# Roots of the first pairs one pair at a time, later v loads behind a later root, their maxima spread through a line of memory, and later batches' value products five units behind the scores

## The chip, the cores and the metric

The kernel is one program on one core of a Trainium2 chip. The metric is the device time of one execution in microseconds, lower is better. The core has a matrix engine (PE, whose weight loads are listed apart as PEld), three engines for elementwise work and reductions (DVE, ACT, POOL), and SP, which here only issues transfers. Every engine, and every queue of transfers, takes its instructions in the order in which the program lists them; an instruction that has to wait holds up all that stand behind it on its engine.

## The reference, cut to what matters

```python
# attention: batch 4, heads 12, seq S = 448, head dim D = 64
q_n, k_n = rmsnorm(q, g_q), rmsnorm(k, g_k)
scores = (1 / sqrt(D)) * q_n @ k_n.transpose(0, 1, 3, 2)
attn = softmax(scores, axis=-1)
x = (attn @ v), laid out as [1792 tokens, 768]
# first feed-forward, w_in [768, 2048], w_out [2048, 768]
h = x @ w_in;  g = h * sigmoid(1.702 * h);  y = g @ w_out
# second feed-forward, its own w_in and w_out of the same shapes
h = y @ w_in2;  g = maximum(h, 0) + alpha * minimum(h, 0);  out = g @ w_out2
```

`rmsnorm(x, g)` is `x / sqrt(mean(x*x) + 1e-6) * g` over the 64 elements of a head.

## The kernel before

**Stages.** Attention works on pairs of heads: NP = 6 pairs in each of the B = 4 batches, four units to a pair. Batch 0 runs first, in f32, while the weights of the first feed-forward arrive as 8-byte words and are rebuilt: `from_words` (ACT L147, DVE L163 and L164), the largest value of each piece (DVE L244) and a split into two 16-bit halves (ACT L178, DVE L179). Then the first feed-forward of batch 0 runs, with the attention of batch 1 filled in between its products, then that of batch 1 with the attention of batch 2, and so on; the second feed-forward comes last. The order of every engine is made by a list scheduler from the program as it is written; the order of a queue is that of its issuing engine.

**The first pairs.** For each pair ACT squares q and k, DVE sums the squares (L403, tile `ss`), POOL turns the sums into reciprocal roots with a first guess and three rounds of four small operations (`normalize`, L404 to L414, tile `rs`), DVE multiplies (L438, tile `qn`), PE transposes (L445, L447, tile `qt`) and ACT brings the result to its place (L448). Then PE makes the scores (L496). `normalize` can take several pairs at once: pairs 0 and 1 have a chain of POOL operations each, pairs 2 and 3 share one, and so do pairs 4 and 5. `rooted[P]` is the last operation of the chain of pair P.

**The later v's.** All of v of batches 1 to 3 is read once in advance for its largest magnitude: `v_scale` loads 8 pieces of 168 KB per batch on POOL's queue (L310) into the two buffers of `vst`, and ACT takes the magnitudes' sum in `t` with a column of results (L311). `v_scales` then reduces the columns on DVE (L299), rounds to a power of two (L104, L105), and `partition_max` spreads the largest over all partitions: a diagonal on DVE (L117, `diag`), a product with ones on PE (L119, `pm`), a maximum on DVE (L120), then a reciprocal (L111, L112). This stands in the program once for batch 0, once for each of batches 1 to 3 and in a few places for weights. The loads may begin after `rooted[1]`. The scale of batch 0's v is needed for `first_sc` (DVE L656), which ACT uses to write `x` (L139), the input of the first product of the feed-forward (PE L727, `hp`).

**Later batches.** For a unit PE makes scores (L505, tile `sp`), DVE the row maximum (L510, `nm`), ACT the exponent (L529, `pr`) and the upper half (L571, `ph`), DVE the lower half (L598), SP issues the transpose of `ph` into `pt` (two buffers), and PE multiplies with v (L626, `xp`). Within `attention` a step is one unit; the values of a pair of units are written LAG_ = 4 steps behind their scores:

```python
last = min(NU, 4 * NP * (b + 2)) + LAG
while done < min(want, NU + LAG):
    next(att_steps)
```

Each batch's feed-forward has 56 ticks over which its attention steps are spread. `yp` (L796) is the second product of the first feed-forward, `hp` of L727 and L773 the first.

Of the kernel before, what the change touches and what calls it, by code (L numbers as in the profile page):

```python
# [9 lines left out]
F32 = mybir.dt.float32  # L10
# [4 lines left out]
ALU = mybir.AluOpType  # L15
# [3 lines left out]
VN = 8  # L19
# [4 lines left out]
W1O_AFTER = 4  # L24
VLAG = 0
LAG_ = 4
PACE = (1.0, 1.0, 1.0, 1.0)
HOLD = 12800
M_AT = 2
# [27 lines left out]
def attention_moe_kernel(  # L57
# [215 lines left out]
    g_col = const.tile([128, 1], F32, name="g_col")  # L273
    mv = const.tile([128, B], F32, name="mv")
    av = const.tile([128, B], F32, name="av")

    def gains():
        gq = small.tile([128, D], F32, tag="gq", name="gq", bufs=1)
# [25 lines left out]
    def v_scale(b):  # L304
        flat = v[b].rearrange("h s d -> (h s d)").rearrange("(p n) -> p n", p=128)
        n = flat.shape[1] // VN
        col = small.tile([128, VN], F32, tag="vcol", name="vcol")
        for i in range(VN):
            t = raw_p.tile([128, n], F32, tag="vst", name="vst")
            nc.gpsimd.dma_start(out=t, in_=flat[:, i * n:(i + 1) * n])  # L310
            nc.scalar.activation(out=t, in_=t, func=AF.Abs, accum_out=col[:, i:i + 1])  # L311
        v_scales(b, col)

    raws = {}
    rawv = {}
# [348 lines left out]

    def attention(us):

        for i in range(len(us) + LAG):
            if 0 < i <= len(us):
                high(us[i - 1])
            if i < len(us):  # L670
                scores(us[i])
                exponent(us[i])
            if 2 <= i <= len(us) + 1:
                low(us[i - 2])
            if i >= LAG and us[i - LAG] % 2 == 1:
                values(us[i - LAG] // 4, us[i - LAG] % 4 // 2)
            yield

    def first_pairs():

        steps = attention([4 * P + r for P in range(NP) for r in range(2)])
        for i, _ in enumerate(steps):
            P, r = divmod(i, 2)
            if P >= NP:
                yield
                continue
            if r == 0:
                prep = prep_pair(P + 1) if P + 1 < NP else iter(())
            next(prep, None)
            if r == 0 and P % 2 == 0 and P + 2 < NP:  # L690
                normalize(P + 2, P + 3)
            if r == 1:
                if P + 1 + QKB < NP:
                    load_qk(P + 1 + QKB)
                if P + 3 < NP:
                    load_v(P + 3)
            yield
# [456 lines left out]
    if True:  # L1154
        make_identity(nc, ident)
        nc.vector.memset(ones, 1.0)
        nc.vector.tensor_copy(out=identf, in_=ident)
        load_qk(0)
        gains()
        load_v(0)  # L1160
        load_qk(1)
        load_v(1)
        g0 = big.tile([128, KF, 2, S], F16, tag="g", name="g0")
        stage = g0.rearrange("p m e t -> p (m e t)").bitcast(F32)
        parts = stage[:, 0:R1I * 1024].bitcast(I32).rearrange("p (i n t) -> p i n t", i=R1I, t=2)
        raw1o = g0.rearrange("p m e t -> p m (e t)").bitcast(I32)[:, KF - 4 * R1O:, FIRST:].rearrange("p m (n t) -> p m n t", t=2)

        def num1i(j):
            if j == KD - 1:
                return stage[:, 5120:5120 + FF]  # L1170
            return held.bitcast(F32)[:, (j - 3) * FF:(j - 2) * FF]

        def num1o(j):
            if j == KF - 2:
                return att_p.tile([128, 2 * NT2 * D], F32, tag="ph", name="num1o", bufs=PHB)[:, 0:DM]
            return raw_p.tile([128, 2 * NT2 * D], F32, tag="qk", name="num1o", bufs=QKB)[:, 0:DM]

        w1i_steps = weights(
            moe_w_in, "w1i", lambda: w1i, later_rows(w1i, 3, num1i), lambda t: parts[:, t % R1I], 4, R1I, 2.0 ** -14, scales,
            G1I  # L1180
        )
        w1o_steps = weights(
            moe_w_out, "w1o", lambda: w1o, later_rows(w1o, 2, num1o), lambda t: raw1o[:, 4 * (t % R1O):4 * (t % R1O) + 4], 2,
            R1O, 2.0 ** -25, scales, G1O
        )
        next(w1i_steps)
        normalize(0)
        for _ in prep_pair(0):
            pass
        for P in range(2, 1 + QKB):  # L1190
            load_qk(P)
        load_v(2)
        normalize(1)
        for _ in first_pairs():
            for _ in range(W_RATE):
                next(w1i_steps, None)
        for _ in w1i_steps:
            pass
        v_scales(0, v0)
        first_x()  # L1200
        moe1_scales(0)
        for P in range(NP, NP + 2):
            load_qk(P)
            load_v(P)
        n1o = 0
        steps = attention([4 * P + r for P in range(NP) for r in range(2, 4)])
        for i, _ in enumerate(steps):
            pairs = max(0, (i - LAG + 1) // 2)
            rows = KF - 2 if pairs >= 4 else (HOLD + pairs * HELD) // (2 * DM) - 2
            while n1o < min(1 + 2 * rows + 3 * (rows // 2), (i + 1) * W1O_RATE, 57):  # L1210
                next(w1o_steps)
                n1o += 1
            if i >= M_AT and i - M_AT < KF:
                first_in(slice(0, FIRST), i - M_AT, g0, None)
            if i == VS_AT:
                for b in range(1, B):
                    with tc.issue_after(rooted[1].ins):
                        v_scale(b)
        while n1o < 57:
            next(w1o_steps)  # L1220
            n1o += 1
        for m in range(len(range(2 * NP + LAG)) - M_AT, KF):
            first_in(slice(0, FIRST), m, g0, None)
        with tc.issue_after(loads["w1o"][W1O_HOLD].ins):
            normalize(NP, NP + 1)
            for _ in prep_pair(NP):
                pass
            load_qk(NP + 2)
            load_qk(NP + 3)
            load_v(NP + 2)  # L1230
        att_steps = other_batches()
        done = 4 * NP
        late = late_weights(ctx, att)
        for b in range(B):
            last = min(NU, 4 * NP * (b + 2)) + LAG
            first = done
            got = None
            for i, _ in enumerate(moe1(b) if b else first_moe1(g0)):
                lead = 0 if b else B1_AT
                want = first + (last - first) * min(1.0, max(0.0, i + 1 - lead) / (PACE[b] * TICKS - lead))  # L1240
                while done < min(want, NU + LAG):
                    next(att_steps)
                    done += 1
                if b == B - 1:
                    for _ in range(1 if i < 2 * KF else 2):
                        if got is None or i >= 2 * KF:
                            got = next(late, None)
        second_layer(late)
# [30 lines left out]
```

## Time and profile before

| | |
|---|---|
| Time, median of 3 runs | 1167.9 us (1166.9 to 1169.97) |
| Profiled execution, its own time | 1169.73 us |
| its span in the trace | 1168.0 us |
| mean granted clock of PE | 0.961 |
| PE, busy share of the span | 92% |
| DVE | 69% |
| ACT | 58% |
| POOL | 15% |

The span is what the trace covers, and the time has 1.73 us more around it. The busy shares are means over stages that differ; times below are counted from the start of the span. A granted clock of 1.00 is 2.4 GHz, and the other level is 1.2 GHz.

### The profile page before, as it was taken

The numbers are of one execution on the slowest core, as the hardware profiler recorded it, in microseconds if no ns is written. First come the engines' busy times: TensorE is split into PE (matmuls) and PEld (weight loads), VectorE is DVE, ScalarE is ACT, GpSimd is POOL, SyncE is SP. The second block draws the span as 40 slices with busy tenths as digits, with TensorE's granted clock in tenths as the row PEclk, the third lists the DMA queues.
The fourth block names the chain that finished last, engine by engine and source line by source line (L and its number), as shares of the span: only waits on it lengthen the run. The fifth ranks groups of instructions, "written<-read, shape, count | busy, mean of one in ns | idle before, by whom it ended". The sixth has DMA issues, their size and how long they took to land.

```text
span 1168.0 us, 18355 instructions
## 1 busy us (share of the span) xinstructions
PE 1072.6 (92%) x6755; PEld 586.6 (50%) x6755; DVE 810.1 (69%) x1407; ACT 682.0 (58%) x1396; POOL 169.6 (15%) x336
## 2 busy tenths in 40 slices
PE   3587779778998999999999999999999999999998
PEld 1243447743444445545555455444444477666665
DVE  6979987897788976567633957499977222978351
ACT  4789666576888886578733554256545323645220
POOL 3321001575543432210000000000000000000000
PEclk9677889998999999999999999999999999999999
DMA  7975542358898876665555801555533413353011
GB/s 244 273 213 143 148 136 71 89 100 165 173 175 171 148 121 143 139 120 97 102 123 155 302 4 52 201 202 195 183 103 120 138 68 120 100 179 105 29 32 31
DMA packets 235274, 158.05 MB, mean 135 GB/s; under 512 B 167728, under 2 KB 214448, under 8 KB 235184
## 3 DMA queue, kind: packets, MB, share of 16 engines
q1 hardware_dynamic: 228912, 141.21, 46.5%
q0 software_dynamic: 6272, 15.67, 5.2%
q8 instruction: 53, 0.87, 0.3%
q14 instruction: 37, 0.30, 0.1%
HBM read 92.22 MB, written 25.69 MB: 101 GB/s over the span
## 4 chain that ended last, share of the span: by engine, by line
PE 49%; DVE 17%; DMA 13%; ACT 10%; issue 7%; POOL 3%; SPq 1%; ACTq 0%; DVEq 0%; POOLq 0%
PE op L1062 16%; PE h L902 10%; PE yp L796 10%; PE hp L773 5%; ACT pr L529 3%; PE xp L626 2%; DVE ph L598 2%; DVE nm L510 2%; DMA w2raw<-in_moe_w_in_dram 2%; DMA g<-in_moe_w_out_dram 2%; ACT ph L571 2%; DVE g L140 1%; DMA t<-hl 1%; PE hp L727 1%; DMA yr<-y_dram 1%
## 5 line engine op out<-in xcount | busy, mean ns | idle before, releaser
L796 PE MATMUL yp<-g,w1o 128*128 128x448 f16 x1152 | 228.3, 356 | 0.6 <-DVE g L737 0.6
L902 PE MATMUL h<-x,w2i 128*128 128x512 f16 (+1 forms) x1152 | 220.6, 354 | 3.5 <-DVE rm_w2o L104 2.2
L773 PE MATMUL hp<-x,w1i 128*128 128x448 f16 x864 | 169.8, 353 | 1.8 <-DVE t L782 1.8
L902 PEld LDWEIGHTS <-w2i 128*128 128x128 f16 x1152 | 113.1, 98 | 110.0 <-issue 6.3
L796 PEld LDWEIGHTS <-w1o 128*128 128x128 f16 x1152 | 110.2, 98 | 112.5 <-issue 14.1
L773 PEld LDWEIGHTS <-w1i 128*128 128x128 f16 x864 | 81.9, 98 | 83.9 <-issue 9.9
L598 DVE SCALAR_TENSOR_TENSOR ph<-pr,sm,ph 128x448 f16<-128x448 f32 x126 | 89.6, 739 | 27.6 <-ACT ph L571 27.4
L510 DVE TENSOR_REDUCE nm<-sp 128x2 f32<-128x896 f32 x96 | 92.5, 964 | 10.5 <-PE sp L505 8.4
L907 ACT ACTIVATE pos<-h,sign 128x512 f32<-128x512 f32 (+1 forms) x64 | 40.1, 628 | 91.8 <-PE h L902 84.7
L529 ACT ACTIVATE pr<-sp,nm,c_s 128x448 f32<-128x448 f32 x126 | 90.1, 718 | 3.8 <-DVE ph L598 2.2
L571 ACT ACTIVATE ph<-pr,sm 128x448 f16<-128x448 f32 x126 | 77.9, 660 | 18.1 <-DVE sm L568 18.0
L1062 PEld LDWEIGHTS <-even 128*128 128x128 f16 x672 | 65.7, 98 | 43.4
L908 DVE SCALAR_TENSOR_TENSOR pos<-h,slope,pos 128x512 f32<-128x512 f32 (+1 forms) x64 | 43.4, 680 | 61.0 <-ACT pos L907 61.0
L727 PE MATMUL hp<-x,w1i 128*128 128x256 f16 (+1 forms) x576 | 63.2, 270 | 10.1 <-DVE g L737 7.6
L1062 PEld LDWEIGHTS <-odd 128*128 128x128 f16 x504 | 49.3, 98 | 32.6
L626 PE MATMUL xp<-pt,vs 128*64 128x256 f16 (+1 forms) x792 | 48.6, 268 | 17.4 <-DMA pt<-ph 15.1
L1062 PE MATMUL op<-w2lo,even 128*128 128x384 f16 x384 | 63.4, 326 | 0.0
L727 PEld LDWEIGHTS <-w1i 128*128 128x128 f16 x576 | 53.8, 102 | 18.5 <-issue 13.8
L505 PE MATMUL sp<-t 64*128 64x448 f16 (+1 forms) x432 | 54.6, 360 | 0.9 <-ACT pr L529 0.9
L626 PEld LDWEIGHTS <-vs 128*64 128x64 f16 x792 | 38.6, 113 | 33.0 <-DMA pt<-ph 14.6
L512 ACT ACTIVATE nm<-nm,c_s 128x2 f32<-128x2 f32 x72 | 20.9, 290 | 47.5 <-DVE nm L510 47.3
L1062 PE MATMUL op<-w2hi,even 128*128 128x384 f16 x288 | 47.5, 326 | 0.0
(239 smaller groups left out, 1650.0 us busy)
## 6 DMA issues: line engine op xcount, KB each, us to landing
g<-in_moe_w_in_dram SPq DMA_DIRECT2D x24, 512.0 KB, 5.4
g<-in_moe_w_out_dram SPq DMA_DIRECT2D x32, 384.0 KB, 3.7
w2raw<-in_moe_w_in_dram SPq DMA_DIRECT2D x24, 512.0 KB, 5.6
w2raw<-in_moe_w_out_dram SPq DMA_DIRECT2D x16, 768.0 KB, 6.3
g_dram<-pos SPq DMA_DIRECT2D x48, 256.0 KB, 2.0
gp<-g_dram SPq DMA_DIRECT2D x8, 1024.0 KB, 7.1
odd<-g_dram SPq DMA_DIRECT2D x6, 1024.0 KB, 5.4
y_dram<-y SPq DMA_DIRECT2D x24, 224.0 KB, 2.6
```

Of the source, the lines that this page charges most:

```text
L505: nc.tensor.matmul(out=sp[:, j, 0:S] if n == 2 else sp[ds, 0, 0:S], lhsT=qt[ds] if n == 2 else qt[ds, 64:128], rhs=kt[ds, 0:S], start=(i = ...
L510: nc.vector.tensor_reduce(out=nm[:, 0:n], in_=sp[:, 0:n, 0:S], op=ALU.max, axis=AX, negate=True)
L529: nc.scalar.activation(out=pr[i], in_=sp[:, i, 0:S], func=AF.Exp, bias=nm[:, i:i + 1], scale=c_s if u >= 4 * NP else 1.0, accum_out=sm[:, ...
L571: nc.scalar.activation(out=ph[:, i, 0:S], in_=pr[i], func=AF.Copy, scale=sm[:, i:i + 1])
L598: nc.vector.scalar_tensor_tensor(out=ph[:, i, S:2 * S], in0=pr[i], scalar=sm[:, i:i + 1], in1=ph[:, i, 0:S], op0=ALU.mult, op1=ALU.subtract)
L626: nc.tensor.matmul(out=xp[64 * j:64 * j + 64, t:t + n], lhsT=vs[ks, j, c], rhs=pt[ks, 7 * j + kc, 0:n] if b else pt[ks, kc, o:o + n], star ...
L727: nc.tensor.matmul(out=ps, lhsT=w1i[:, kk, e, m * 128:(m + 1) * 128], rhs=xs[0, kk][:, f, cols], start=(i == 0), stop=(i == 3 * KD - 1))
L773: nc.tensor.matmul(out=ps, lhsT=w1i[:, kk, e, m * 128:(m + 1) * 128], rhs=x[:, f], start=(n == 0), stop=(n == 3 * KD - 1))
L796: nc.tensor.matmul(out=ps, lhsT=w1o[:, m, e, j * 128:(j + 1) * 128], rhs=g[:, m, f], start=(n == 0), stop=(n == 3 * KF - 1))
L902: nc.tensor.matmul(out=ps, lhsT=w2i[:, kk, e, m * 128:(m + 1) * 128], rhs=x2[kk][:, f], start=(c == 0), stop=(c == 3 * KD - 1))
L908: nc.vector.scalar_tensor_tensor(out=pos, in0=ps, scalar=slope[:, m:m + 1], in1=pos, op0=ALU.mult, op1=ALU.max)
L1062: nc.tensor.matmul(out=ps, lhsT=ops[:, o, m, f], rhs=rhs[:, e], start=(c == 0), stop=(c == 3 * KH - 1))
```

## The change

The roots of pairs 2 to 5 are made one pair at a time. The 24 loads of later v's may begin after `rooted[4]` in place of `rooted[1]`. Their columns are kept in one tile `vcols`, and the maxima of the three batches are made together: one reduction, one rounding, one write of 128 x 3 values to a line of memory (SP), one read of that line by all partitions (SP, tile `vrow` in a buffer of `sq`), one maximum and one reciprocal. In later batches values stand five steps behind scores, and are written ahead of the lower halves in a step; the number of steps by which attention runs ahead of the feed-forward is one higher too.

```diff
+LAG2 = 5
...
     def v_scale(b):
...
-        col = small.tile([128, VN], F32, tag="vcol", name="vcol")
+        col = vcols[:, b - 1]
         for i in range(VN):
             t = raw_p.tile([128, n], F32, tag="vst", name="vst")
             nc.gpsimd.dma_start(out=t, in_=flat[:, i * n:(i + 1) * n])
             nc.scalar.activation(out=t, in_=t, func=AF.Abs, accum_out=col[:, i:i + 1])
-        v_scales(b, col)
+
+    def later_v_scales():
+        n = B - 1
+        one = small.tile([128, B - 1], F32, tag="vone", name="vmax")
+        nc.vector.tensor_reduce(out=one, in_=vcols, op=ALU.max, axis=AX)
+        pow2floor(one, one)
+        line = dram.tile([128, n], F32, name="v_line")
+        row = att_p.tile([128, 128 * n], F32, tag="sq", name="vrow", bufs=SQB)
+        nc.sync.dma_start(out=line, in_=one)
+        nc.sync.dma_start(out=row, in_=line.rearrange("p b -> (p b)").partition_broadcast(128))
+        nc.vector.tensor_reduce(out=mv[:, 1:B], in_=row.rearrange("q (p b) -> q b p", b=n), op=ALU.max, axis=AX)
+        scaled_reciprocal(av[:, 1:B], mv[:, 1:B], 2.0 ** 13)
...
     def attention(us):
 
+        LAG = LAG_ if us[0] < 4 * NP else LAG2
         for i in range(len(us) + LAG):
...
-            if 2 <= i <= len(us) + 1:
-                low(us[i - 2])
-            if i >= LAG and us[i - LAG] % 2 == 1:
-                values(us[i - LAG] // 4, us[i - LAG] % 4 // 2)
+            late = us[0] >= 4 * NP
+            for what in (1, 0) if late else (0, 1):
+                if what == 0 and 2 <= i <= len(us) + 1:
+                    low(us[i - 2])
+                if what and i >= LAG and us[i - LAG] % 2 == 1:
+                    values(us[i - LAG] // 4, us[i - LAG] % 4 // 2)
             yield
...
-            if r == 0 and P % 2 == 0 and P + 2 < NP:
-                normalize(P + 2, P + 3)
+            if r == 0 and P + 2 < NP:
+                normalize(P + 2)
...
                 for b in range(1, B):
-                    with tc.issue_after(rooted[1].ins):
+                    with tc.issue_after(rooted[4].ins):
                         v_scale(b)
+                later_v_scales()
...
-            last = min(NU, 4 * NP * (b + 2)) + LAG
+            last = min(NU, 4 * NP * (b + 2)) + LAG2
...
-                while done < min(want, NU + LAG):
+                while done < min(want, NU + LAG2):
```

Lines of the changed kernel stand 13 lines later than before around the roots and the units (L404 is L417, L438 is L451, L505 is L518, L626 is L639), and one or two later near its start (L119 is L120, L164 is L165, L310 is L312).

**POOL, first pairs.** Before, after the chain of pair 1 (its last operation writes `rs` at 128x14), four loads of later v stand ahead of the chain that pairs 2 and 3 share (128x28), and one more inside it:

```order
L414 TENSOR_TENSOR rs<-tn,rs 128x14
L310 DMA vst<-in_v_dram 128x336 x4
L404 TENSOR_SCALAR ss<-ss 128x28
...
L413 TENSOR_SCALAR tn<-tn 128x28
L310 DMA vst<-in_v_dram 128x336
L414 TENSOR_TENSOR rs<-tn,rs 128x28
L310 DMA vst<-in_v_dram 128x336 x3
```

Now the chains of pairs 2, 3 and 4 follow directly; these rows are the end of the chain of pair 4 and what comes behind it, the chain of pair 5 in between:

```order
L425 TENSOR_TENSOR tn<-tn,ss 128x14
L426 TENSOR_SCALAR tn<-tn 128x14
L427 TENSOR_TENSOR rs<-tn,rs 128x14
L312 DMA vst<-in_v_dram 128x336 x4
L417 TENSOR_SCALAR ss<-ss 128x14
...
L427 TENSOR_TENSOR rs<-tn,rs 128x14
L312 DMA vst<-in_v_dram 128x336 x20
```

All 24 loads have moved behind the fifth chain; the first stood behind the second chain before.

**DVE, up to the third pair's `qn`.** The first piece is before, the second of the changed kernel; `w1i` is a piece of the first weights, `ss` the sums of squares:

```order
L510 TENSOR_REDUCE nm<-sp 128x2
L163 TENSOR_SCALAR w1i<-w1i 128x512
L164 SCALAR_TENSOR_TENSOR w1i<-g_143,w1i 128x512 x2
L179 SCALAR_TENSOR_TENSOR w1i<-w1i,inv_w1i 128x2048
L450 TENSOR_REDUCE v_96<-w1o 128x1
L163 TENSOR_SCALAR w1i<-w1i 128x512
L403 TENSOR_REDUCE ss<-sq 128x7 x2
L163 TENSOR_SCALAR w1i<-w1i 128x512
L438 TENSOR_TENSOR qn<-qk,rs 128x2x7x64
```

```order
L523 TENSOR_REDUCE nm<-sp 128x2
L164 TENSOR_SCALAR w1i<-w1i 128x512
L165 SCALAR_TENSOR_TENSOR w1i<-g_144,w1i 128x512
L463 TENSOR_REDUCE v_97<-w1o 128x1
L451 TENSOR_TENSOR qn<-qk,rs 128x2x7x64
L416 TENSOR_REDUCE ss<-sq 128x7
L165 SCALAR_TENSOR_TENSOR w1i<-g_144,w1i 128x512
L180 SCALAR_TENSOR_TENSOR w1i<-w1i,inv_w1i 128x2048
L416 TENSOR_REDUCE ss<-sq 128x7
```

The `qn` of the third pair now stands ahead of one split of 128x2048 (L179 before), of the two sums of squares of the fifth pair and of one L163, all of which stood ahead of it.

**PE, where three products for later maxima stood** (between the f32 scores of the second half of batch 0's pairs and the transposes `tp` of their probabilities), before and now:

```order
L496 MATMUL sp<-t_540 128x448 x2
L119 LDWEIGHTS ones
L119 MATMUL pm<-diag,ones 128x128
L496 MATMUL sp<-t_540 64x448 x2
L119 LDWEIGHTS ones
L119 MATMUL pm<-diag,ones 128x128
L119 LDWEIGHTS ones
L119 MATMUL pm<-diag,ones 128x128
L586 MATMUL tp<-identf,pr 128x128 x4
```

```order
L509 MATMUL sp<-t_552 128x448 x2
L599 MATMUL tp<-identf,pr 128x128 x2
L509 MATMUL sp<-t_552 64x448 x2
L599 MATMUL tp<-identf,pr 128x128 x2
L565 MATMUL rp<-identf,sums 64x128 x2
```

The three products with ones are gone from PE.

**PE, scores and values of a later pair.** Numbers tell the units apart; `sp` are the scores of three following units, `xp` the values of one pair, whose two halves come from two `pt`. The pieces leave out the rows of the feed-forward and of repeats; before, then now:

```order
L505 MATMUL sp_2819<-t1_2559 128x448
...
L626 MATMUL xp_2838<-pt_2660,vs_2425 64x256
...
L505 MATMUL sp_2886<-t1_2559 128x448
...
L626 MATMUL xp_2838<-pt_2763,vs_2425 64x192
...
L505 MATMUL sp_2923<-t1_2559 64x448
```

```order
L518 MATMUL sp_2817<-t1_2569 128x448
...
L518 MATMUL sp_2872<-t1_2569 128x448
...
L639 MATMUL xp_2888<-pt_2670,vs_2435 64x256
...
L518 MATMUL sp_2933<-t1_2569 64x448
...
L639 MATMUL xp_2888<-pt_2761,vs_2435 64x192
```

Each group of values has moved behind one more group of scores.

## Rows read from the trace of the kernel before

**Rows 1.** Windows: length, busy (x) of PE, PEld, DVE, ACT, POOL; clock, DMA share, GB/s.

```profile
22.00:126.00 104.00, 70.14 (x354) 35.46 (x353) 91.93 (x187) 81.71 (x195) 22.79 (x50) 0.75 0.74 212
126.00:243.00 117.00, 98.67 (x836) 73.75 (x836) 98.97 (x226) 79.16 (x180) 27.83 (x51) 0.90 0.38 100
243.00:290.00 47.00, 37.94 (x253) 18.39 (x253) 36.12 (x50) 32.01 (x78) 27.18 (x36) 0.89 0.76 150
290.00:410.00 120.00, 111.17 (x825) 55.40 (x823) 100.41 (x167) 102.43 (x248) 54.57 (x106) 0.99 0.88 167
410.00:620.00 210.00, 210.00 (x1445) 106.21 (x1444) 129.68 (x216) 142.95 (x333) 28.12 (x59) 1.00 0.61 119
```

**Rows 2.** Waits of PE: waited for, us in total, times, longest.

```profile
PE xp L626 <- DMA pt<-ph: 15.1, 10, 3.6
PE qt L445 <- DVE qn L438: 14.6, 3, 11.0
```

**Rows 3.** Timeline of PE near 43: start, duration, instruction, [idle before <- releaser].

```profile
43.04 0.88 PE L445 MATMUL qt<-identf,qn 128*128 128x128 f32 x3 [11.04 <-DVE qn L438]
```

**Rows 4.** Timeline of DVE, 31 to 43.

```profile
31.93 1.13 DVE L403 TENSOR_REDUCE ss<-sq 128x7 f32<-128x448 f32 x2
...
35.52 2.34 DVE L179 SCALAR_TENSOR_TENSOR w1i<-w1i,inv_w1i 128x2048 f16<-128x2048 f32 x1
...
41.80 1.09 DVE L438 TENSOR_TENSOR qn<-qk,rs 128x896 f32<-128x896 f32 x1 [1.63 <-POOL rs L414]
```

**Rows 5.** Timeline of POOL: the first chain's ends, and the third and fourth pairs' shared chain.

```profile
9.38 0.26 POOL L404 TENSOR_SCALAR ss<-ss 128x14 f32<-128x14 f32 x1 [8.08 <-DVE ss L403]
...
13.29 0.22 POOL L414 TENSOR_TENSOR rs<-tn,rs 128x14 f32<-128x14 f32 x1
...
33.15 0.28 POOL L404 TENSOR_SCALAR ss<-ss 128x28 f32<-128x28 f32 x1 [3.99 <-DVE ss L403]
...
34.13 1.57 POOL L412 TENSOR_TENSOR tn<-tn,ss 128x28 f32<-128x28 f32 x1
35.78 2.15 POOL L413 TENSOR_SCALAR tn<-tn 128x28 f32<-128x28 f32 x1
...
41.51 0.26 POOL L414 TENSOR_TENSOR rs<-tn,rs 128x28 f32<-128x28 f32 x1
```

**Rows 6.** Timeline of POOL: issues of the 9th and the 24th load of later v.

```profile
59.85 0.61 POOL L310 DMA_DIRECT2D vst<-in_v_dram  x1 [3.67 <-ACT vst L311]
...
105.83 0.54 POOL L310 DMA_DIRECT2D vst<-in_v_dram  x1 [4.02 <-ACT vst L311]
```

**Rows 7.** Timeline of ACT: one wait for such a load, and the write of x.

```profile
70.70 0.48 ACT L311 ACTIVATE vst<-vst 128x336 f32<-128x336 f32 x1 [3.92 <-DMA vst<-in_v_dram]
...
125.38 0.89 ACT L139 ACTIVATE x<-xraw,first_sc 128x256 f16<-128x256 f32 x2
```

**Rows 8.** Timeline of PE, 164 to 172.

```profile
169.01 0.27 PE L119 MATMUL pm<-diag,ones 128*128 128x128 bf16 x1 [3.08 <-DVE diag L117]
171.54 0.26 PE L119 MATMUL pm<-diag,ones 128*128 128x128 bf16 x1 [2.27 <-DVE diag L117]
```

**Rows 9.** Timeline of DVE: one maximum over partitions.

```profile
116.92 0.29 DVE L120 TENSOR_REDUCE mv<-pm 128x1 f32<-128x128 f32 x1 [0.44 <-PE pm L119]
```

**Rows 10.** Transfers: queue, count, KB each, median us from issue to landing.

```profile
row<-line SPq DMA_DIRECT2D x3, 64.0 KB, 4.4
...
line<-am SPq DMA_DIRECT2D x1, 0.5 KB, 9.3
```

**Rows 11.** Timeline of PE: the first second product of the feed-forward, and value products.

```profile
243.10 3.75 PE L796 MATMUL yp<-g,w1o 128*128 128x448 f16 x19 [0.64 <-DVE g L737]
...
253.71 1.39 PE L626 MATMUL xp<-pt,vs 128*64 128x256 f16 x22 [2.00 <-DMA pt<-ph]
...
262.17 0.27 PE L626 MATMUL xp<-pt,vs 128*64 128x192 f16 x1 [1.75 <-DMA pt<-ph]
...
265.00 1.92 PE L626 MATMUL xp<-pt,vs 128*64 128x192 f16 x21 [1.58 <-DMA pt<-ph]
```

More of the change, by code (lines that the diff above doesn't have):

```diff
@@ L275, in attention_moe_kernel @@
     av = const.tile([128, B], F32, name="av")
+    vcols = const.tile([128, B - 1, VN], F32, name="vcols")
     def gains():
```

## The prediction, made before the changed kernel was run

> **What bounds the kernel now.** I read the windows by stage first, then PE's waits, then the timelines around the longest of them. From 410 on PE is busy for the whole of its window (210.00 of 210.00 us, [rows 1]), so what is won or lost before 410 moves the end by as much, and what is won after it is small. Before 410 the kernel has two parts with different limits.
>
> The first ends with the first `yp`, at 243.10 [rows 11]. From 22 to 243 PE is busy for 168.8 of 221 us and DVE for 190.9 [rows 1], 86%. DVE is the fullest engine, but its idle time, 221 - 190.9 = 30.1 us, leaves room for a wait to be removed. PE's largest single wait there is 11.04 us for `qn` of the third pair, before the transpose at 43.04 [rows 3].
>
> In the second, from 243 to 410, PE is idle for (47 - 37.94) + (120 - 111.17) = 17.9 us [rows 1]. Its waits for `pt` come to 15.1 us in ten [rows 2], all in this stretch: the first three are 2.00, 1.75 and 1.58 us [rows 11], 5.3 together, and the other seven 15.1 - 5.3 = 9.8. DVE is busy for 36.12 of 47 and 100.41 of 120 us here, ACT for 102.43 of 120 [rows 1]. So PE's gaps can be closed to a degree before these two become the limit.
>
> **The roots.** The third pair's `qn` starts at 41.80, when the shared chain's last operation at 41.51 is done [rows 4, 5]. That chain starts at 33.15, when the fourth pair's sums are done, and lasts 8.6 us. A chain of one pair took 13.29 + 0.22 - 9.38 = 4.1 us [rows 5]. On POOL the third pair's chain now waits for that pair's sums alone, which stand ahead of the fourth's at 31.93 [rows 4], so its root is ready by 31.93 + 4.1 = 36.0 at the latest, before DVE gets to `qn`. DVE's list decides then. In it the split (2.34 us), the fifth pair's two sums (1.13 as in the row of the fourth's) [rows 4] and one L163 have moved behind `qn`, and the wait of 1.63 us for POOL [rows 4] falls away: 2.34 + 1.13 + 1.63 = 5.1 us, and with the L163, which I do not count, somewhat more. `qn` comes at about 36.7 instead of 41.8. PE, which waited 11.04 us, starts its transposes 5.1 us sooner.
>
> Not all of this reaches 243. The moved DVE work of 3.5 us must still be done there; only the wait of 1.63 us is DVE time regained for certain. PE and ACT chains start up to 5.5 us earlier (5.1 and the L163). The bounds are thus -1.6 and -5.5. I take -3, nearer to DVE's end since DVE is 86% busy, and above it since 30.1 us of its time are waits that an earlier start of the other engines can fill.
>
> At one place rows show two lengths of one operation: L412 took 1.57 us and L413 2.15 beside DVE's L164 and split of 35.52, against 0.22 for the 14-wide L414 [rows 4, 5]. The Trainium skill, "GPSIMD Engine Reference", section "1. Specifications", says that GpSimd shares its SBUF interfaces with VectorE, which contends when DVE reads two SBUF inputs; both DVE operations do, and the trace agrees with 1.57 and 2.15 us. By that rule the new, more numerous small operations can each be held as well, and the root of the fifth pair comes later than I count.
>
> **The later v's loads.** Before, the first stands behind the second chain and ACT works through them while pairs are made. Now all 24 stand behind the fifth chain. The fifth pair's sums follow `qn` of the third at 36.7, behind that `qn` (1.09), one L164 and the split (2.34) [rows 4]: about 42, and with 4.1 us for the chain the first load is issued at about 46. ACT takes them in its list, in order, 23 of them before it writes the first `x`, at 125.38 before [rows 7]. From the 9th to the 24th, 15 issues took 105.83 - 59.85 = 45.98 us [rows 6], 3.07 each, with two buffers. At that pace the 23rd is issued at 46 + 22 x 3.07 = 113.5 and used up to 3.92 us later [rows 7], 117.5. This is ahead of 125.4, so I cost the later start at 0. The ends: POOL and ACT no longer carry loads between 20 and 46, when PE starves, up to -4 (about one wait of ACT for a load, 3.92 [rows 7]); and a list that bunches these loads up ahead of `x` can make ACT wait for one more, +5 (3.92 and the 0.6 us of an issue [rows 6], rounded up).
>
> **The maxima.** Three products with ones leave PE. Two of them waited 3.08 and 2.27 us at 169.01 and 171.54 [rows 8], with f32 scores queued behind them on PE and nothing else there able to go: 5.4 us. What DVE did in those 5.4 us it still does, and the scores' consumers queue on DVE. Bounds 0 and -5.4; I take -3, past the middle, since PE's list from 126 to 243 is 84% full at a clock of 0.90 [rows 1] and can use the time at once. DVE loses three maxima of 0.29 us [rows 9] and three diagonals of the same shape, 1.7 us by that row, and gains one reduction over three times the elements, 0.9 by the same row: -0.8, which counts because DVE is the full engine.
>
> The line of memory costs transfers on SP: one write like the row of 9.3 us, one read like that of 4.4 [rows 10]. They stand among the loads of the first `w_out`, 11 of these ahead of the write, 8 between it and the read and 11 behind. The write hides behind its 8 loads, which wait for DVE to free buffers in any case. After the read is issued, DVE has in its list some six operations ahead of the maximum that needs it, about as long as one L403 (1.13 / 2 = 0.6 us [rows 4]), an estimated 3.6 us, so it stalls for about 4.4 + 0.4 (waking up) - 3.6 = 1.2 us; all of DVE's list stands behind. Bounds 0 (DVE is late itself) and +3. I take +1.2.
>
> First part: -3 + 0 - 3 - 0.8 + 1.2 = -5.6.
>
> **Five units behind.** Between the last `ph` of a pair and its values there is now one more unit, and the time of a step, (410 - 243) / 28 = 6.0 us, is more than the longest of these waits, 3.6 [rows 2]. The first three waits stay: the first values of batch 1 come after the same six groups of scores in both lists, because nothing was ahead of them. So up to 9.8 us can go. Two `pt` buffers are kept; a transpose that waits for values to release a buffer does so more often in the new list (27 of 90 against 22), and gives part back. I take -7. Against it, 29 steps instead of 28 fall in the first stretch, 243 to 410, where a step costs DVE at most 136.5 / 28 = 4.9 us, all its other work included, and DVE is 82% busy (136.5 of 167 us, [rows 1]); I take somewhat under half of it, since the rest fits in idle time of DVE: +2. That work is missing from the next stretch, but PE is full there and gains nothing. Sum -5, bounds -9.8 and +4.9 (the waits stay and the step is paid whole).
>
> **Sum.** 1169.73 - 5.6 - 5 = 1159.1 against the profiled execution, whose span of 1168.0 has 1.73 us around it. That execution lies 1.83 us above the median of 1167.9; against the median the forecast is 1157.3, I write 1157.
>
> **Rivals.** 0.3% of the median, about 3.5 us, is what a measurement of this kernel can tell from no change.
>
> *Both parts pay* (0.45): 1157, its own range 1151 to 1163.
>
> *DVE's list before 243 is full* (0.15). The roots give 1.6, the maxima nothing but their 0.8, the line takes 1.2: -1.2; with -5, 1167.9 - 6.2 = 1162. For it speaks 88% of DVE in the window from 22 to 126 (91.93 of 104 [rows 1]); against it PE's waits of 11.04, 3.08 and 2.27, for which DVE's order, not its amount of work, is to blame.
>
> *The lag gives nothing* (0.12). The two `pt` buffers move the wait from values to the transpose and on to the next unit's `ph`: -5.6 alone, 1162.
>
> *Neither pays* (0.15). DVE's list keeps the first `yp` at 243 and the buffers keep the waits: within 1164.4 to 1171.4, about 1167.
>
> *Slower: the loads arrive after `x` is due* (0.13). The loads start at 46 rather than 20, with 23 ahead of `x` on ACT. It decides at (125.4 - 3.92 - 46) / 22 = 3.4 us per load; the pace before was 3.07. At 4 us each the 23rd is used at 46 + 88 + 3.92 = 138, 12.5 us late; with -5 from the lag, 1167.9 + 12.5 - 5 = 1175.4. Where every small chain between 33 and 46 is held by DVE as the shared one was (1.57 and 2.15 us in place of 0.22 each, 3.3 us per chain [rows 5]), the start goes to about 46 + 2 x 3.3 = 52.6, the 23rd at the old pace to 124.1, and the margin is gone. By the rule of the skill named above this would be the usual case wherever DVE reads two inputs. Against it: ACT would have them in a row, and without waiting for other work a load needs only its own transfer.
>
> **Numbers.** Faster by over 0.3%: 0.45 + 0.15 + 0.12 = 0.72. Within: 0.15. Slower: 0.13. The range is 1147 to 1171. Below, the bounds leave 2.5 (roots), 2.4 (maxima), 4 (loads) and 4.8 us (lag), 13.7 in all, which do not all come true together; I go down by 10. Above it reaches to the far end of "neither pays". Outside remain most of the slower case and a few in a hundred of the rest.
>
> **What would show it.** PE's wait for the third pair's `qn` falls from 11.04 to about 6, and `qn` starts near 37 behind DVE's own work, not behind POOL. The first load of later v is issued near 46, the 23rd is used before 120, and the write of `x` comes at or before 125. The waits at 169 are gone, and the first `yp` comes near 237.5. DVE waits about 1 us for `vrow`. Waits of PE for `pt` fall to about 8 us, of which the first three keep 5. I am wrong if ACT's waits for `vst` grow to several of 3.92 us, if `yp` stays at 243 with a fuller DVE, or if DVE or ACT waits for `pt`'s buffers where PE waited before.

## The result, and the profile after

The changed kernel takes 1152.7 us (median of 6, 1148.73 to 1156.94) against 1168.93 of before in the same comparison (1166.23 to 1171.63): ratio 0.9863, 95% interval 0.9836 to 0.9891, 16 us faster. The forecast was 1157, with a range of 1147 to 1171. The profiled execution has a span of 1149.9 us, 18.1 less than before. The page's first part and its row of the granted clock (each digit is one fortieth of the span, in tenths of full speed, 9 for 90% or more):

```profile
span 1149.9 us, 18349 instructions
...
PE 1058.2 (92%) x6752; PEld 579.9 (50%) x6752; DVE 804.3 (70%) x1392; ACT 680.6 (59%) x1396; POOL 176.7 (15%) x364
...
PEclk9677999999989999999999999999999999999999
```

Of the 18.1 us, 14.4 are PE's busy time (1072.6 before, 1058.2 now) and 3.7 its idle time, though PE has only three products fewer. The windows, cut at the same events as [rows 1] (the first `x`, the first `yp`; columns as there):

```profile
22.00:119.00 97.00, 64.45 (x344) 34.03 (x344) 84.44 (x159) 75.68 (x181) 32.48 (x80) 0.74 0.75 212
119.00:229.30 110.30, 92.85 (x844) 69.73 (x843) 102.72 (x238) 84.20 (x194) 30.04 (x51) 0.99 0.45 124
229.30:276.00 46.70, 39.55 (x288) 19.44 (x286) 37.83 (x56) 35.97 (x86) 29.23 (x40) 0.99 0.78 157
276.00:396.00 120.00, 109.39 (x799) 53.93 (x798) 97.44 (x162) 100.25 (x246) 49.44 (x103) 0.96 0.79 166
```

The stage from the first `x` to the first `yp` has a granted clock of 0.99 where it had 0.90 [rows 1], and it is 6.7 us shorter (110.3 against 117); the stage ahead of it is 7 us shorter. PE's waits, and the timelines of PE, DVE (the third pair's `qn`, then `first_sc`), ACT (first `x`), POOL (the fifth pair's chain, then the first load of later v):

```profile
PE xp L639 <- DMA pt<-ph: 13.5, 7, 4.5
...
PE qt L458 <- DVE qn L451: 9.2, 3, 5.7
```

```profile
37.56 0.88 PE L458 MATMUL qt<-identf,qn 128*128 128x128 f32 x3 [5.68 <-DVE qn L451]
...
229.29 3.08 PE L812 MATMUL yp<-g,w1o 128*128 128x448 f16 x14
```

```profile
36.33 1.09 DVE L451 TENSOR_TENSOR qn<-qk,rs 128x896 f32<-128x896 f32 x1
...
115.91 0.23 DVE L669 TENSOR_SCALAR first_sc<-ratio_w1i,av 128x6 f32<-128x6 f32 x1
...
152.97 0.68 DVE L324 TENSOR_REDUCE mv<-vrow 128x3 f32<-128x384 f32 x1 [1.09 <-DMA vrow<-v_line]
```

```profile
118.39 1.29 ACT L140 ACTIVATE x<-xraw,first_sc 128x256 f16<-128x256 f32 x3
```

```profile
42.94 0.26 POOL L417 TENSOR_SCALAR ss<-ss 128x14 f32<-128x14 f32 x1
...
48.60 0.22 POOL L427 TENSOR_TENSOR rs<-tn,rs 128x14 f32<-128x14 f32 x1
48.75 1.34 POOL L312 DMA_DIRECT2D vst<-in_v_dram  x2
```

The third pair's transposes start 5.5 us earlier than in [rows 3], the first `x` 7.0 earlier than in [rows 7], the first `yp` 13.8 earlier than in [rows 11]. One sign that was to speak against the forecast is there too: ACT's waits for later v's loads grew (before, then now).

```profile
ACT vst L311 <- DMA vst<-in_v_dram: 6.3, 6, 3.9
...
ACT vst L313 <- DMA vst<-in_v_dram: 14.3, 7, 3.7
```

### The profile page after: what moved, and what is told of

Read it like the earlier page. It is cut to its first block, busy times and chain, and to the rows that moved or that the text cites. A ratio compares the mean times of both kernels' runs of the same rounds, so it can differ in the third digit from the quotient of the medians.

```text
span 1149.9 us, 18349 instructions
## 1 busy us (share of the span) xinstructions
PE 1058.2 (92%) x6752; PEld 579.9 (50%) x6752; DVE 804.3 (70%) x1392; ACT 680.6 (59%) x1396; POOL 176.7 (15%) x364
## 4 chain that ended last, share of the span: by engine, by line
PE 55%; DVE 16%; DMA 9%; issue 9%; POOL 5%; ACT 5%; SPq 1%; ACTq 0%; POOLq 0%; DVEq 0%
PE op L1078 17%; PE yp L812 13%; PE h L918 11%; PE hp L789 8%; PE xp L639 2%; PE sp L518 2%; DMA t<-hl 2%; DVE ph L611 2%; DMA vst<-in_v_dram 1%; DMA pt<-ph 1%; DVE ss L416 1%; DVE nm L523 1%; DVE g L141 1%; PE hp L743 1%; ACT pr L542 1%
## 5 line engine op out<-in xcount | busy, mean ns | idle before, releaser
L812 PE MATMUL yp<-g,w1o 128*128 128x448 f16 x1152 | 225.4, 353 | 0.4 <-DVE g L141 0.4
L611 DVE SCALAR_TENSOR_TENSOR ph<-pr,sm,ph 128x448 f16<-128x448 f32 x126 | 85.5, 712 | 18.6 <-ACT ph L584 18.4
L584 ACT ACTIVATE ph<-pr,sm 128x448 f16<-128x448 f32 x126 | 77.4, 658 | 13.8 <-DVE sm L581 13.4
L639 PE MATMUL xp<-pt,vs 128*64 128x256 f16 (+1 forms) x792 | 49.7, 268 | 14.8 <-DMA pt<-ph 13.5
L518 PE MATMUL sp<-t 64*128 64x448 f16 (+1 forms) x432 | 54.7, 360 | 3.0 <-ACT pr L542 3.0
L639 PEld LDWEIGHTS <-vs 128*64 128x64 f16 x792 | 37.6, 112 | 33.5 <-issue 15.3
```

Of the source, the lines that this page charges most:

```text
L518: nc.tensor.matmul(out=sp[:, j, 0:S] if n == 2 else sp[ds, 0, 0:S], lhsT=qt[ds] if n == 2 else qt[ds, 64:128], rhs=kt[ds, 0:S], start=(i = ...
L584: nc.scalar.activation(out=ph[:, i, 0:S], in_=pr[i], func=AF.Copy, scale=sm[:, i:i + 1])
L611: nc.vector.scalar_tensor_tensor(out=ph[:, i, S:2 * S], in0=pr[i], scalar=sm[:, i:i + 1], in1=ph[:, i, 0:S], op0=ALU.mult, op1=ALU.subtract)
L639: nc.tensor.matmul(out=xp[64 * j:64 * j + 64, t:t + n], lhsT=vs[ks, j, c], rhs=pt[ks, 7 * j + kc, 0:n] if b else pt[ks, kc, o:o + n], star ...
L812: nc.tensor.matmul(out=ps, lhsT=w1o[:, m, e, j * 128:(j + 1) * 128], rhs=g[:, m, f], start=(n == 0), stop=(n == 3 * KF - 1))
```

## The experiments

Ratios are to the kernel before, run beside each. For each kernel two numbers are read beside its ratio: how many operations on pieces of `w_out` (`from_words`, L163 and L164 before, on `w1o`) DVE's list has ahead of `first_sc`, and, from PE's timeline, the end of the last f32 value product, where batch 0's attention ends. The last two columns come from the one profiled execution of a kernel, which can lie off its median: loads_alone 1173.10 us against 1180.92, pm_late 1165.48 against 1160.36, no_spread 1162.67 against 1167.18.

| kernel | ratio (95%) | `w_out` operations ahead | `first_sc` at | batch 0's attention ends |
|---|---|---|---|---|
| before | 1 | 31 | 124.0 | 197.4 |
| changed | 0.9863 (0.9836 to 0.9891) | 22 | 115.9 | 182.5 |
| roots_alone | 1.0087 (1.0059 to 1.0114) | 24 | 121.8 | 196.5 |
| spread_alone | 0.9836 (0.9816 to 0.9857) | 22 | 115.9 | 181.4 |
| lag_alone | 1.0041 (1.0019 to 1.0063) | 31 | 124.2 | 197.4 |
| loads_alone | 1.0102 (1.0074 to 1.0130) | 35 | 128.2 | 199.7 |
| pm_late | 0.9925 (0.9894 to 0.9955) | 31 | 125.8 | 190.0 |
| no_roots | 0.9988 (0.9966 to 1.0011) | 35 | 130.4 | 197.1 |
| no_loads | 0.9925 (0.9896 to 0.9953) | 30 | 128.1 | 194.4 |
| no_lag | 0.9865 (0.9831 to 0.9899) | 22 | 114.3 | 181.2 |
| merged_pm | 0.9939 (0.9914 to 0.9963) | 22 | 117.4 | 191.9 |
| spread_late | 0.9908 (0.9882 to 0.9935) | 22 | 116.6 | 180.0 |
| no_spread | 0.9990 (0.9960 to 1.0020) | 23 | 116.3 | 189.4 |
| spread_lag | 0.9897 (0.9851 to 0.9942) | 22 | 117.1 | 181.9 |

**Each part alone.** roots_alone:

```diff
-            if r == 0 and P % 2 == 0 and P + 2 < NP:
-                normalize(P + 2, P + 3)
+            if r == 0 and P + 2 < NP:
+                normalize(P + 2)
```

> The kernel before with one change, roots of pairs 2 to 5 one pair at a time. Theory 1 (the terms add up as the prediction has them): the wait of 11.04 us for qn of the third pair falls to about 6, and -3 us, ratio 0.997. Theory 2 (the first half of batch 0 is limited by other work and gives the 5 us back; most of the 14 us before the first yp came from the maxima): qn comes as early, but the first x stays near 125 and the time moves by under 1.5 us, ratio 0.999 to 1.001. Theory 3 (the parts need each other, above all loads and roots): no part alone moves the time by more than 3 us.

Slower by 10 us, which none of the three expected. PE's wait for the third pair's `qn` fell from 11.04 [rows 3] to 4.34 us, and the first `x` came 2 us earlier:

```profile
36.74 0.87 PE L458 MATMUL qt<-identf,qn 128*128 128x128 f32 x3 [4.34 <-DVE qn L451]
```

But batch 0's attention ended at 196.5, 0.9 earlier than before, so nearly all was given back by there, and between 290 and 430 ACT waited for the q and k of later pairs (before, in the same stretch: 4.8 us in four waits):

```profile
ACT sq L414 <- DMA qk<-in_q_dram: 13.9, 3, 6.1
```

DVE waited behind it for the squares (12.7 us against 1.7). POOL's queue has another order there, which the edit does not name; why the scheduler made it so, and how much of the 10 us these waits are, was not tried.

spread_alone, on the kernel before (and `later_v_scales()` as in the change):

```diff
-        v_scales(b, col)
...
+                later_v_scales()
```

> The kernel before with one change, the later maxima through a line of memory, loads still behind the second chain. Theory 1: -2.6 us (3 for the two waits of 3.08 and 2.27, 0.8 of DVE, less 1.2 for the read), ratio 0.998. Theory 2: with the waits near 169 gone PE's granted clock does not fall to 0.5 there, the stage from the first x to the first yp runs at 0.98 or more in place of 0.90, and the gain is 8 us or more, ratio 0.993 or less. Theory 3: under 3 us.

Faster by 19 us: the whole gain of the change and a little more, and far beyond theory 1's 2.6. Theory 2 has the size right and its condition wrong: from the first `x` to the first `yp` the granted clock is 0.94, above the 0.90 of before but short of 0.98 (columns as in [rows 1]):

```profile
117.00:239.00 122.00, 98.84 (x866) 74.62 (x866) 108.25 (x241) 87.62 (x201) 34.41 (x56) 0.94 0.52 127
```

The clock is not the only thing that changed: the first `x` came at 116.72 and no longer at 125.38. The profile of this kernel still has the wait of 11.04 us for the third pair's `qn`:

```profile
PE qt L458 <- DVE qn L451: 14.6, 3, 11.0
```

So that wait, the longest in [rows 2], is not what the time hangs on.

lag_alone (with the place of values ahead of the lower halves, as in the change):

```diff
+LAG2 = 5
...
+        LAG = LAG_ if us[0] < 4 * NP else LAG2
...
-            last = min(NU, 4 * NP * (b + 2)) + LAG
+            last = min(NU, 4 * NP * (b + 2)) + LAG2
```

> The kernel before with one change, values of later batches five steps behind scores (with their place ahead of the lower halves and the attention's one more step of lead). Theory 1: -5 us, waits for pt from 15 to 8, ratio 0.996. Theory 2: the waits for pt stay (13.5 us in seven in the changed kernel against 15.1 in ten), -1 to -2 us, ratio 0.999. Theory 3: under 3 us.

Slower by 4.8 us. PE's waits for `pt` did not go (15.1 us in ten before [rows 2]); they became more and shorter:

```profile
PE xp L639 <- DMA pt<-ph: 16.4, 13, 3.3
```

loads_alone:

```diff
-                    with tc.issue_after(rooted[1].ins):
+                    with tc.issue_after(rooted[4].ins):
```

> The kernel before with one change, the loads of later v behind the root of the fifth pair (which here is in one chain with the sixth's). Theory 1: 0 (-4 to +5), ACT's waits for these loads grow from 6 us to 10 or more without a later x. Theory 2: the same. Theory 3: slower by 3 us or more, since without separate roots the fifth root comes near 64 and the last loads are used after 130.

Slower by 12 us, as theory 3 had it in size. ACT's waits for q and k of later pairs grew as with the roots alone (10.2 us), and `first_sc` stands behind 35 operations on `w_out` and comes at 128.2.

**The changed kernel without a part, and the maxima in other places.** pm_late leaves the later maxima on PE, written behind the second half of batch 0:

```diff
-        v_scales(b, col)
...
+        for b in range(1, B):
+            v_scales(b, vcols[:, b - 1])
         with tc.issue_after(loads["w1o"][W1O_HOLD].ins):
```

> The kernel before, with the three later maxima still spread by products with ones on PE, but written behind the second half of batch 0 (on PE they stand some 340 rows later); loads, roots and lag as before. DVE's list ahead of first_sc is as long as before (205 operations; with the line of memory alone it was 187). Theory A (most of the spread's gain came from work that moved behind first_sc on DVE): first x stays near 125, the waits near 169 go, and the gain is 5 us, ratio 0.995 to 0.998. Theory B (the gain came from PE's waits near 169 and the clock that falls behind them): 12 us or more, ratio under 0.99, clock of the stage from x to the first yp 0.97 or more. Theory C (only the line of memory with its one maximum does it): within 2 us of before.

Faster by 8.6 us, between theories A and B. `first_sc` stays behind its 31 operations and the first `x` comes no earlier (127.24), so nothing of these 8.6 us comes from an earlier `first_sc`. The waits near 169 are not gone: they stand near 203, behind the end of batch 0's attention, with 4.4 us in place of 5.35:

```profile
202.64 0.22 PE L120 MATMUL pm<-diag,ones 128*128 128x128 bf16 x1 [1.22 <-DVE diag L118]
206.04 0.26 PE L120 MATMUL pm<-diag,ones 128*128 128x128 bf16 x1 [3.18 <-DVE diag L118]
```

PE's clock falls around them here too, and from the first `x` to the first `yp` it is 0.90 as before, where theory B wanted 0.97 (the last row is that stage):

```profile
200.00:206.00 6.00, 1.64 (x15) 1.27 (x13) 5.55 (x16) 1.63 (x3) 2.73 (x10) 0.82 0.00 1
206.00:212.00 6.00, 5.96 (x46) 5.59 (x46) 5.74 (x21) 3.49 (x5) 3.43 (x5) 0.61 0.64 148
...
128.00:251.70 123.70, 105.06 (x900) 77.15 (x898) 107.34 (x240) 90.37 (x209) 33.70 (x57) 0.90 0.43 112
```

So this run moves the waits and does not take them away, and what its 8.6 us come from is not shown.

no_roots (the changed kernel, `normalize(P + 2, P + 3)` again):

> The changed kernel with the shared chains of before for pairs 2 to 5. Theory A (roots, loads and lag each cost time, alone and together): faster than the changed kernel, ratio to before 0.985 or less. Theory B (the loads' later place costs only where the fifth root is late, and roots pay that back): slower, first x 4 us or more later, ratio 0.990 to 0.995.

All of the gain is gone (0.9988): theory B's direction, at more than its price. The loads wait for a fifth root that is late: the first of them is issued here at 58.27, and PE's first `hp` comes at 133.5 (125.92 before).

no_loads (`rooted[1]` again):

> The changed kernel with the loads of later v behind the second chain again. Theory A: faster than the changed kernel by some us, ratio to before 0.980 to 0.985, ACT's waits for these loads 6 us in place of 14. Theory B: the loads break up the chains of POOL and hold back the third pair's qn; the same or slower than the changed kernel, 0.986 to 0.990.

Slower than the changed kernel by 0.6%: theory B's direction, at more than its figure. POOL's chains are not held back (PE waits 4.15 us for the third pair's `qn`); but `first_sc` moved back behind 30 operations, to 128.1.

no_lag (`LAG2 = 4`, and the order of values and lower halves as before):

> The changed kernel with values four units behind scores as before. Theory A (the lag alone cost 4 us): faster, ratio to before 0.982 or so, and PE's waits for pt no more than 13.5 us. Theory B (the prediction's term): slower by 5 us, ratio 0.990, waits for pt 18 us or more.

0.9865 against the changed kernel's 0.9863, in four executions with an interval of 4 us to either side: within that the lag is worth nothing here. PE's waits for `pt` are 14.4 us in nine without it, 13.5 in seven with it.

**What in the maxima pays.** merged_pm, on the kernel before, reduces the three together and spreads them by three products with ones (the edit is in `later_v_scales` of the changed kernel):

```diff
+        for b in range(1, B):
+            partition_max(mv[:, b:b + 1], one[:, b - 1:b])
-        line = dram.tile([128, n], F32, name="v_line")
...
-        nc.vector.tensor_reduce(out=mv[:, 1:B], in_=row.rearrange("q (p b) -> q b p", b=n), op=ALU.max, axis=AX)
```

> The kernel before with the three later maxima reduced together on DVE, in one tile, and then spread by three products with ones on PE as before (no line of memory); loads, roots and lag as before. DVE's list ahead of first_sc is as with the line of memory alone (22 operations on pieces of w_out ahead of it; before 31), and the three products stand on PE where they stood. Theory A (what counts is how much of w_out's rebuild DVE does ahead of first_sc): first x near 117, the end of batch 0's attention on PE near 185, 1150 to 1156 us, ratio 0.985 to 0.990; the waits of PE for diag cost 3 to 5 us of what the line gave. Theory B (PE's waits near 169 are what counts): ratio 0.995 or more.

Faster by 7 us, short of theory A's range and beyond theory B's. The first `x` is as early as with the line of memory, and the waits for `diag` are still there, 9 and 7 us earlier than in [rows 8], and longer, 7.3 us against 5.35:

```profile
159.84 0.22 PE L120 MATMUL pm<-diag,ones 128*128 128x128 bf16 x1 [2.47 <-DVE diag L118]
164.85 0.27 PE L120 MATMUL pm<-diag,ones 128*128 128x128 bf16 x1 [4.79 <-DVE diag L118]
```

Behind them PE's clock falls to its lower level, in the windows of this kernel (columns as in [rows 1]):

```profile
156.00:162.00 6.00, 1.58 (x8) 0.48 (x7) 5.09 (x16) 3.28 (x7) 0.00 (x0) 0.91 0.07 21
162.00:168.00 6.00, 3.07 (x19) 2.05 (x20) 5.95 (x16) 2.16 (x6) 0.00 (x0) 0.50 0.64 177
168.00:174.00 6.00, 5.78 (x38) 3.73 (x37) 4.70 (x16) 3.35 (x6) 0.00 (x0) 0.74 0.60 179
```

spread_late writes `later_v_scales()` behind the second half of batch 0:

> The kernel before with the maxima through a line of memory, written behind the second half of batch 0, so that the maximum of the line stands some 60 places later on DVE. Theory A: as with the line alone, 1146 to 1150 us, ratio 0.982 to 0.985, and DVE's wait of about 1 us for the line gone. Theory B: the same. A third: that wait was worth more than 1 us, ratio under 0.981.

1156.42 us, less of a gain than with the line at its place, which none of the three had. DVE waits 1.2 us for the line here; in the profile of spread_alone it does not wait for it at all. Batch 0's attention ends as early as in any kernel (180.0).

no_spread (the changed kernel, maxima as before):

> The changed kernel with the later maxima one batch at a time through products with ones on PE, as before. 23 operations on pieces of w_out stand ahead of first_sc on DVE. Theory A (the place of first_sc is what counts): first x near 118 to 121, 1153 to 1160 us, ratio 0.988 to 0.993. Theory B (the line of memory is what counts): ratio 0.998 to 1.005.

0.999: theory B's figure, though the first `x` comes at 118, as theory A said. PE's waits for `diag` are 11.8 us here, the largest of its list, but only the last two of these three rows are for later v's; the first is for the weights' maximum:

```profile
PE pm L120 <- DVE diag L118: 11.8, 3, 6.3
...
109.41 0.29 PE L120 MATMUL pm<-diag,ones 128*128 128x128 bf16 x1 [6.34 <-DVE diag L118]
...
162.34 0.27 PE L120 MATMUL pm<-diag,ones 128*128 128x128 bf16 x1 [3.83 <-DVE diag L118]
164.22 0.27 PE L120 MATMUL pm<-diag,ones 128*128 128x128 bf16 x1 [1.61 <-DVE diag L118]
```

These two come to 5.4 us, as in [rows 8].

spread_lag (line of memory and lag of five):

> The line of memory and the lag of five, with roots and loads as before. 22 operations on pieces of w_out ahead of first_sc. Theory A: first x near 117, 1147 to 1153 us, ratio 0.983 to 0.988, so that roots and loads together are worth nothing beside these two. Theory B: the lag costs 4 to 5 us as it did alone, 1152 us.

0.9897 with an interval of 0.9851 to 0.9942: outside theory A's range, which the interval reaches, and 1154.48 us is nearer to theory B's 1152. On top of these two, the roots make it 0.9925 (no_loads), the loads 0.9988 (no_roots) and both 0.9863 (changed): the later loads alone take back all that the line gives, the roots alone cost no more than the intervals allow for chance, and together they are at most worth a few tenths of a per cent.

## Why the prediction came out right, and where its steps did not

The time lies in the range and the direction is right, but that the sum of -10.6 us came near the measured -16 is luck: one term was far too small, and others that were counted as gains gave none.

**The maxima, -3 (bounds 0 to -5.4): the step that was mis-sized.** Alone they measure -19 us (0.9836, interval 0.9816 to 0.9857), and without them the other parts give nothing (no_spread, 0.9990). Two things were left out. First, "DVE loses three maxima" counted those operations and the diagonals alone. The scheduler also rearranged what stands ahead of `first_sc`: 22 operations on `w_out` instead of 31, and the first `x` 7 to 9 us earlier. In merged_pm, where the products stay on PE, `first_sc` comes at 117.4 and the time falls by 7 us although PE's waits for `diag` are longer. Second, a wait of PE was priced at its own length. Around the two waits of [rows 8] the kernel before has these windows, and the changed kernel the next:

```profile
162.00:168.00 6.00, 3.92 (x27) 2.15 (x25) 3.93 (x14) 3.23 (x9) 0.00 (x0) 0.99 0.34 110
168.00:174.00 6.00, 2.03 (x12) 1.13 (x11) 6.00 (x15) 3.28 (x7) 0.00 (x0) 0.50 0.70 197
174.00:180.00 6.00, 6.00 (x42) 4.26 (x42) 3.85 (x18) 1.82 (x6) 0.00 (x0) 0.65 0.24 66
```

```profile
162.00:168.00 6.00, 4.98 (x44) 3.78 (x42) 5.70 (x17) 5.32 (x13) 0.00 (x0) 1.00 0.82 223
168.00:174.00 6.00, 5.10 (x50) 3.85 (x50) 5.90 (x13) 3.99 (x9) 0.00 (x0) 1.00 0.45 129
174.00:180.00 6.00, 2.90 (x26) 2.20 (x22) 5.27 (x13) 4.48 (x10) 0.08 (x1) 1.00 0.65 174
```

Before, PE is busy 2.03 of 6 us, DVE all of it, and the clock is at 0.50, the lower level, and then 0.65 while PE is full. So the matmuls behind the wait take longer too, and PE gets through 81 (of several kinds) in 18 us where it now gets through 120 in the same window, though not of the same work. An estimate from these rows: at a clock of 1.00 the 2.03 and 6.00 us of PE's work in the last two windows would take 2.03 x 0.50 + 6.00 x 0.65 = 4.9 us, 3.1 less, so that the two waits of 5.35 us cost about 8.5 with the clock behind them. No run takes only the waits away: pm_late moves them, with a fall of the clock, and no_loads, without them and with `first_sc` as late as 128.1, is 9 us faster than before but has the roots and the lag too. So how the 19 us divide among an earlier `x`, the waits and the clock is not shown. How much the products off PE give beyond merged_pm is not settled either: 3.6 us by spread_late, 12 by spread_alone.

**The roots, -3.** `qn` at 36.33 (forecast 36.7) and PE's wait of 5.68 us (forecast about 6) are right to half a microsecond; the worth is wrong. Alone they cost 10 us. Where they are taken out of the changed kernel nearly 15 us are lost (0.9988 against 0.9863), but only 4 where the later place of the loads goes with them (spread_lag, 0.9897): so the loss comes from the later loads without separate roots, where the fifth root is late. They have no worth of their own that could be put into a sum.

**The loads, 0 (-4 to +5).** The first is issued at 48.75, where 46 was forecast. A chain of one pair was reckoned at 4.1 us [rows 5]; the fourth pair's took 42.76 + 0.22 - 34.73 = 8.2, so that the fifth's began 0.9 us late, and the fifth's took 48.60 + 0.22 - 42.94 = 5.9. These rows are of POOL in the fourth pair's chain (its start, a long operation, its end) and in the fifth's, then of DVE:

```profile
34.73 0.53 POOL L417 TENSOR_SCALAR ss<-ss 128x14 f32<-128x14 f32 x1
...
38.69 2.19 POOL L425 TENSOR_TENSOR tn<-tn,ss 128x14 f32<-128x14 f32 x1
...
42.76 0.22 POOL L427 TENSOR_TENSOR rs<-tn,rs 128x14 f32<-128x14 f32 x1
...
45.36 1.11 POOL L426 TENSOR_SCALAR tn<-tn 128x14 f32<-128x14 f32 x1
```

```profile
38.46 2.34 DVE L180 SCALAR_TENSOR_TENSOR w1i<-w1i,inv_w1i 128x2048 f16<-128x2048 f32 x1
...
45.32 1.08 DVE L451 TENSOR_TENSOR qn<-qk,rs 128x896 f32<-128x896 f32 x1
```

Each of the two long POOL operations ends 0.07 to 0.08 us after the DVE operation beside it (40.88 and 40.80, 46.47 and 46.40). The Trainium skill, "GPSIMD Engine Reference", section "1. Specifications", names contention with VectorE instructions that have two SBUF inputs, as these two have; the trace agrees, with 4.1 and 1.8 us more for the two chains. The prediction's slower rival reckoned 3.3 for each of two.

Alone the loads measure +12 us, outside the bounds; beside the other three -7 (0.9925 without them, 0.9863 with them), beyond -4 by its middle but not by more than the two intervals leave open. The forecast of the 23rd load was right: it is used at 117.91, where 117.5 was forecast, since the later start was made up by a quicker pace.

```profile
117.91 0.48 ACT L313 ACTIVATE vst<-vst 128x336 f32<-128x336 f32 x1 [1.68 <-DMA vst<-in_v_dram]
```

What changed is when `x` is due. `first_sc` is ready at 115.91 + 0.23 = 116.14, and the first `x` is written at 118.39, right behind this load. The rival that ends slower was right that ACT waits for these loads (14.3 us where it was 6.3) and that they come to stand last ahead of `x`; it was wrong in the size, for they hold `x` up by some 2 us at most, with a `first_sc` that comes 8 us earlier.

**The line of memory, +1.2.** The wait measured 1.09 us of DVE's time at 152.97, close to the forecast. What it is worth in the kernel's time is not shown: 1.2 us of it stand in spread_late, none in spread_alone.

**The lag, -5 (-9.8 to +4.9).** Alone +4.8, in the changed kernel 0. The step that fails is "up to 9.8 us can go": waits for `pt` were 13.5 us in seven where about 8 were forecast. The rival that the buffers only move the wait fits lag_alone, with thirteen waits in place of ten. The stage behind the first `yp` is 18.1 - 13.8 = 4.3 us shorter than before, close to the forecast 5. In the profile of no_lag that stage is not shorter, 1153.1 - 227.5 = 925.6 us against 1149.9 - 229.3 = 920.6 with the lag and 924.9 before, but its first `yp` comes 1.8 us earlier:

```profile
227.49 3.65 PE L812 MATMUL yp<-g,w1o 128*128 128x448 f16 x14
```

So in these two executions the lag moves 5 us out of the last stage and gives part back ahead of it; of the difference that is left, 3 us, the medians show 1.3 (1154.02 against 1152.7), less than the intervals can tell. And lag_alone, with a first `yp` at 243.44 and a span of 1168.5, leaves that stage at 925.1.

**What goes with the time** in the fastest kernels is where batch 0's attention ends on PE. It ends between 180.0 and 182.5 in the five kernels that have the early `first_sc` and the line of memory, and these are the five of the lowest times (0.9836 to 0.9908). Among the others the two go together only loosely: it ends at 189.4 in no_spread, 8 us earlier than before, with the time of before (0.9990), and at 194.4 in no_loads with 0.9925. That the place of `first_sc` causes this and does not only go with it was not tried by moving it alone. Two rivals stand. One is the order of PE's list, which was not tried by itself without the three products. The other is ACT's list: before, ACT writes the first `x` at 125.38, more than 1 us after `first_sc`, behind an operation on `w_out` that had waited for its load.

```profile
124.93 0.54 ACT L147 ACTIVATE w1o<-g 128x384 f32<-128x384 f32 x1 [1.25 <-DMA g<-in_moe_w_out_dram]
```

## What to carry to other kernels

Where a list scheduler sets the order, read what each list has ahead of the operation that a stage waits for, before and after, and price the work that moved across it; here nine operations on `w_out` that the diff does not name left the list ahead of `first_sc`, and the first `x` came 7 us earlier. Price a wait of the matrix engine with the granted clock of the windows behind it, and not only by its own length (here an estimated 8.5 us for 5.35). Parts that share a queue or a list are not a sum: try them alone and left out, for the later place of the loads measured +12 us alone and -7 beside the others.

## What the runs showed that was not expected

A fast start of PE was worth little by itself here: the wait of 11.04 us was cut to 4.34 with a loss of 10 us, and left whole with a gain of 19. And most of the 18.1 us between the two profiled executions are PE's busy time (14.4), with three products with ones fewer that take about 0.25 us each; the granted clock of the stage from the first `x` to the first `yp` went from 0.90 to 0.99. That clock does not order the kernels: spread_alone, the fastest, has 0.94 there, and pm_late, faster by 8.6 us, 0.90. Two small operations of the roots on POOL lasted 2.19 and 1.11 us instead of 0.22, each beside a DVE operation on two tensors, and ended just after it.
